# Batch one of a fused attention and mixer kernel: the second pair's q and k turned on TensorE, nine steps masked by VectorE, mixing pair by pair

## The chip, the cores and the metric

The kernel runs on one core of a Trainium2 chip. Its time is the device time of one launch in microseconds, the median over the runs. A profiled execution also has a span, from its first to its last recorded instruction. All times inside an execution are counted from the start of that span.

## What is computed

Block-sparse attention over 4 batches, 8 heads, 768 tokens and a head size of 64, followed by a mixer over the 512 channels. The first half, cut to what matters:

```python
scores = scale * np.matmul(q, k.transpose(0, 1, 3, 2))
# mask: neighbouring blocks of 32 tokens, the first and the last block,
# and three sampled blocks for each block of queries
scores = np.where(mask, scores, -1000000000.0)
attn = exp(scores - max) / sum
x = attn @ v                         # then heads side by side: (4, 768, 512)
```

The second half, with U of 768x32 and V of 32x768, w_ch1 of 512x2048 and w_ch2 of 2048x512:

```python
h = xt @ U @ V                       # xt: x with tokens and channels swapped
u = x + h.transpose(0, 2, 1)
ch = np.maximum(u @ w_ch1, 0.0) @ w_ch2
return u + ch
```

The mask is the same for all batches and heads.

## The kernel before

**Units of work.** Two heads make a pair; there are 4 pairs in a batch (pairs 0 to 3 are batch one, pair 4 begins batch two) and 9 steps in a pair, 144 steps in all, numbered through. A step makes the scores of one 128-key tile against 512 queries for both heads (the first six steps of a pair, two matmuls of 64x512), or of two key tiles against the remaining 256 queries (the last three, four matmuls of 64x256), with keys on the partitions. `score` then lets ScalarE take the exp of the whole 128x1024 PSUM tile into an SBUF tile `e`. `values` multiplies each `e` with v, eight matmuls of 65 columns a step; the 65th column is the sum for the softmax. When half of a pair's queries is complete, `divide` takes the reciprocal on VectorE and writes the normalised half as float32 (`x32`) and float16 (`x16`).

**Two ways to mask.** In a *biased* step two more matmuls (or four, for the 256-wide kind) add -60000 to forbidden scores inside PSUM, from the tiles `bias` and `qhot`. In an unbiased step the exp runs on plain scores, and VectorE afterwards multiplies `e` with a 0/1 `mask` (`apply_masks`), before `values` may read it. `build_bias` makes the bias; `build_allow` and `spread` make the mask in pieces. Before the change steps 2 to 35 are biased; steps 0, 1 and 36 to 143 are masked by VectorE.

**Turning q and k.** q and k come by DMA on SP's queue as float32 (`raw_q`, `raw_k`), are narrowed to float16 (`narrow_part`, `narrow_pair`: tiles `st_q`, `st_k`) and turned so that the head size lies on the partitions (`qT`, `kT`). For pair 0 TensorE turns them (`prepare_part`, `transpose_part`) into PSUM and another engine copies them out; for all later pairs a transposing DMA on SP's queue does it (`transpose_by_dma`, called by `prepare_next` together with the loads of the pair after). SP's queue and POOL's work strictly in order: a transposing DMA that waits for its narrowed source holds up the loads that stand behind it.

**Mixing.** `amix` multiplies `x16` with U, `umix` makes u turned (`uT`, one tile per 128 channels, that is per pair) by adding `x16` turned against the identity and V times the amix result in PSUM, and copies it out. In batches two to four only the last pair is done so; the others add in natural layout (`unat`) and turn by DMA. `channels` then runs the two large layers: `up` (pieces `j`, `part`, `half`; w_ch1 and relu into `tT`) and `down` (w_ch2, added to `x32`, stored).

**Order.** One loop writes down all instructions of all engines, choosing at each turn among the next scores ("qk"), values ("av"), mixing pieces and channel pieces. It keeps a model clock per engine (`clk`; `FIX`, `COL`, `HOP` are its costs in ns) and takes the candidate with the best rank among those that its clock holds to be ready. The clock sets only the order and which engine does a copy (`pick`); on the chip everything waits on semaphores.

**PSUM.** While batch one's attention runs (`ahead[0]` true) PSUM is cut into two score tiles of two banks (`sc`) and four single banks (`one`): accumulators of a pair, transposes, amix and umix. When all of batch one is mixed, `all_to_two` closes these pools and opens one of four two-bank tiles (`two`). So step k's scores wait for the exp of step k-2. The stretch up to this re-cut is called the first stage; it contains the scores and exps of steps 0 to 37.

Batch one is mixed in two groups: pairs 0 to 2 together (one amix of 384 columns and three umix), then pair 3. Pair 3's `divide` is ordered reciprocal, `x16`, `x32` for each half.

## Time and profile before

| | |
|---|---|
| median of three runs | 291.26 us (290.24 to 292.35) |
| the profiled execution | 291.53 us, span 289.70 us |
| TensorE busy, 2791 matmuls | 279.0 us, 96% of the span |
| ScalarE busy | 187.9 us, 65% |
| VectorE busy | 159.8 us, 55% |
| POOL busy | 63.6 us, 22% |
| granted TensorE clock | 1.00 |
| exp of 128x1024 | 106 on `two` (1026 ns mean), 38 on `sc` (1040 ns) |
| mask of 128x1024 on VectorE | 74 and 36 (750 and 752 ns mean) |

How to read it: TensorE's busy share includes the pipelined tails of matmuls, so 96% doesn't say that it never waits inside the first stage. The busy shares are means over stages with different limits; for the first stage the exps of ScalarE and the gaps between them tell more. A line of the timeline gives the start, the length of the merged group, the engine, the source line, what is written from what, how many instructions were merged and, in brackets, how long the engine sat idle before them and what released it. PE is TensorE, ACT ScalarE, DVE VectorE. L413 and L420 are the score and bias matmuls, L428 the exp, L504 the values, L603 and L608 the copies of `uT`, L665 and L694 the channel layers.

### The profile page before, as it was taken

The numbers are of one execution on the slowest core, as the hardware profiler recorded it, in microseconds if no ns is written. First come the engines' busy times: TensorE is split into PE (matmuls) and PEld (weight loads), VectorE is DVE, ScalarE is ACT, GpSimd is POOL, SyncE is SP. The second block draws the span as 40 slices with busy tenths as digits, with TensorE's granted clock in tenths as the row PEclk, the third lists the DMA queues.
The fourth block names the chain that finished last, engine by engine and source line by source line (L and its number), as shares of the span: only waits on it lengthen the run. The fifth ranks groups of instructions, "written<-read, shape, count | busy, mean of one in ns | idle before, by whom it ended". The sixth has DMA issues, their size and how long they took to land.

```text
span 289.7 us, 6483 instructions
## 1 busy us (share of the span) xinstructions
PE 279.0 (96%) x2791; PEld 159.1 (55%) x2791; DVE 159.8 (55%) x262; ACT 187.9 (65%) x217; POOL 63.6 (22%) x81
## 2 busy tenths in 40 slices
PE   7998998999899999999999998999999999999995
PEld 2554654566464655566566455566655455565444
DVE  5562256775957665675687666666755743000112
ACT  4898988796957746877965476859786533664000
POOL 4655644501304043004006503004010100000000
PEclk9999999999999999999999999999999999999999
DMA  7799999999952858361626955712110311000122
GB/s 214 193 203 207 237 230 204 281 201 215 156 164 54 242 126 218 98 196 27 141 80 69 268 143 187 217 48 55 29 29 0 102 72 75 0 2 0 54 86 80
DMA packets 52212, 37.68 MB, mean 130 GB/s; under 512 B 33424, under 2 KB 50624, under 8 KB 52184
## 3 DMA queue, kind: packets, MB, share of 16 engines
q1 hardware_dynamic: 46672, 32.71, 43.5%
q0 software_dynamic: 5152, 4.39, 9.6%
q8 instruction: 22, 0.36, 0.6%
q10 hardware_dynamic: 360, 0.17, 0.2%
q14 instruction: 6, 0.05, 0.1%
HBM read 27.59 MB, written 6.29 MB: 117 GB/s over the span
## 4 chain that ended last, share of the span: by engine, by line
PE 86%; ACT 5%; DMA 5%; DVE 1%; issue 1%; POOL 0%; SPq 0%; ACTq 0%; POOLq 0%
PE two L665 29%; PE two L694 28%; PE two L504 9%; PE two L413 8%; ACT e L428 4%; DMA raw_k<-in_k_dram 3%; PE sc L413 3%; PE one L504 2%; DMA kT<-st_k 2%; PE sc L420 2%; PE two L575 1%; PE two L722 1%; PE two L618 1%; PE two L700 1%; ACT uT L608 1%
## 5 line engine op out<-in xcount | busy, mean ns | idle before, releaser
L428 ACT ACTIVATE e<-two 128x1024 f16<-128x1024 f32 x106 | 100.7, 1026 | 19.4 <-PE two L413 19.3
L665 PE MATMUL two<-uT,w1t 128*128 128x256 f16 (+1 forms) x512 | 88.3, 326 | 0.4 <-ACT uT L608 0.2
L694 PE MATMUL two<-w2t,tT 128*128 128x512 f16 x368 | 86.9, 379 | 0.0
L665 PEld LDWEIGHTS <-w1t 128*128 128x128 f16 x512 | 48.2, 98 | 34.9 <-issue 5.7
L461 DVE TENSOR_TENSOR e<-e,mask 128x1024 f16<-128x1024 f16 x74 | 53.4, 750 | 9.3 <-ACT e L428 9.1
L694 PEld LDWEIGHTS <-tT 128*128 128x128 f16 x368 | 33.1, 98 | 39.1 <-issue 5.9
L504 PEld LDWEIGHTS <-e 128*128 128x128 f16 x1152 | 38.3, 97 | 11.8 <-issue 8.4
L682 ACT ACTIVATE tT<-two 128x1024 f16<-128x1024 f32 x31 | 31.7, 1023 | 16.8 <-PE two L665 16.8
L428 ACT ACTIVATE e<-sc 128x1024 f16<-128x1024 f32 x38 | 36.3, 1040 | 4.6 <-PE sc L420 3.5
L708 DVE TENSOR_TENSOR of<-x,two 128x1024 f32<-128x1024 f32 (+1 forms) x12 | 14.1, 1176 | 42.8 <-PE two L700 42.6
L627 POOL CAST x<-x 128x768 f16<-128x768 f32 x9 | 8.1, 900 | 121.9 <-DVE x L624 121.9
L413 PE MATMUL two<-qT,kT 64*128 64x512 f16 (+1 forms) x284 | 29.9, 324 | 2.5 <-DVE uT L603 1.1
L551 ACT CAST x<-x 128x384 f16<-128x384 f32 x24 | 12.3, 512 | 30.1 <-DVE x L537 30.1
L680 DVE TENSOR_SCALAR tT<-two 128x1024 f16<-128x1024 f32 x17 | 20.8, 1225 | 19.7 <-PE two L665 19.7
L413 PEld LDWEIGHTS <-kT 64*128 64x128 f16 x384 | 17.3, 94 | 24.2 <-issue 15.2
L466 DVE TENSOR_TENSOR e<-e,mask 128x1024 f16<-128x1024 f16 x36 | 26.2, 752 | 3.6 <-ACT e L428 3.5
L504 PE MATMUL two<-v,e 128*128 128x65 f16 x864 | 28.2, 193 | 0.0
L413 PE MATMUL sc<-qT,kT 64*128 64x512 f16 (+1 forms) x100 | 16.0, 331 | 1.7 <-DMA kT<-st_k 1.2
L163 POOL CAST st_q<-raw_q 128x768 f16<-128x768 f32 x15 | 12.7, 844 | 22.0 <-DMA raw_q<-in_q_dram 16.1
L154 POOL CAST v<-raw_v 128x768 f16<-128x768 f32 x16 | 14.9, 932 | 5.2 <-DMA raw_v<-in_v_dram 4.8
L163 POOL CAST st_k<-raw_k 128x768 f16<-128x768 f32 x15 | 13.9, 926 | 7.2 <-DMA raw_k<-in_k_dram 6.8
L420 PE MATMUL sc<-qhot,bias 64*128 64x256 f16 (+1 forms) x92 | 14.4, 320 | 0.0
(75 smaller groups left out, 156.1 us busy)
## 6 DMA issues: line engine op xcount, KB each, us to landing
raw_v<-in_v_dram SPq DMA_DIRECT2D x16, 384.0 KB, 5.9
raw_q<-in_q_dram SPq DMA_DIRECT2D x15, 384.0 KB, 4.2
raw_k<-in_k_dram SPq DMA_DIRECT2D x15, 384.0 KB, 4.5
out_dram<-of SPq DMA_DIRECT2D x11, 512.0 KB, 3.3
w1t<-in_moe_w_ch_dram POOLq DMA_DIRECT2D x4, 512.0 KB, 8.8
w2t<-in_moe_w_ch_dram POOLq DMA_DIRECT2D x4, 512.0 KB, 10.5
raw_q<-in_q_dram SPq DMA_DIRECT2D x1, 256.0 KB, 2.9
raw_k<-in_k_dram SPq DMA_DIRECT2D x1, 256.0 KB, 4.2
```

The costliest lines, as they stand in the source:

```text
L154: nc.gpsimd.tensor_copy(out=vs[n % VB][:, :, :, 0:D], in_=raw["v", n].rearrange("p h (t d) -> p t h d", d=D))
L163: nc.gpsimd.tensor_copy(out=st, in_=raw[name, n].rearrange("p h (t d) -> p t h d", d=D))
L413: nc.tensor.matmul(sc[:, h, at : at + nq], kT[h * D : (h + 1) * D, g * P : (g + 1) * P], qT[h * D : (h + 1) * D, q0 : q0 + nq], start=True ...
L420: nc.tensor.matmul(sc[:, h, at : at + nq], biasf[h * D : (h + 1) * D, g : S : NT], qhot[h * D : (h + 1) * D, q0 : q0 + nq], start=False, s ...
L428: nc.scalar.activation(out=e, in_=sc, func=AF.Exp, scale=0.125)
L461: nc.vector.tensor_mul(out=e, in0=e, in1=m)
L466: nc.vector.tensor_mul(out=ev, in0=ev, in1=m)
L504: nc.tensor.matmul(acc[1][hf][:, t % (NT // 2), h, :], e[:, h, at + t * P - q0 : at + t * P - q0 + P], vt[:, g, h, 0 : D + 1], start=(done ...
L665: nc.tensor.matmul(pt[:, half, at : at + nq], w1t[:, c, (4 * j + i) * P : (4 * j + i + 1) * P], uT[c][:, q0 : q0 + nq], start=(c == 0), st ...
L680: nc.vector.tensor_scalar_max(out=dst, in0=pt, scalar1=0.0)
L682: nc.scalar.activation(out=dst, in_=pt, func=AF.Relu)
L694: nc.tensor.matmul(po[:, i], tT[j // 4][:, j % 4, t * P : (t + 1) * P], w2t[:, j, :], start=(j == 0), stop=False,)
```

## The change

Ten edits, all on batch one's stage but for the last lines of `up`, which concern every batch:

1. Of pair 0's k, columns 2 and 3 are narrowed by VectorE instead of POOL, ahead of `bias`, and copied out of PSUM by VectorE instead of ScalarE.
2. Pair 1's q and k are turned on TensorE at steps 6 and 7; its two transposing DMAs go. `spread` follows at step 7 instead of 3, its second part at step 14 instead of 16.
3. Steps 21 to 23 and 27 to 32 become unbiased and are masked by VectorE.
4. Pair 0's values are taken in the order of steps 2 to 8, 0, 1 (before: 2 to 5, 0, 1, 6 to 8).
5. Each half of a pair is divided when its own matmuls are complete.
6. Pair 3's two `x32` products are put off (`later`) until the last `uT` piece has been copied.
7. Batch one is mixed by single pairs, and `umix` is cut into a piece of 512 and one of 256 columns.
8. The first channel pieces (`j` and `part` 0) multiply channels 0 to 2 for both halves, and channels 3 in the second piece.
9. The planner stops scoring at step 37 until the re-cut, and ranks scores otherwise.
10. Model costs: `FIX` of ScalarE 180 instead of 400 ns, `HOP` by engine.

The diff, cut to its core:

```diff
-    def build_bias():
+    def count_allowed():
...
+    def build_bias():
...
-    FIX = {"ACT": 400, "DVE": 350, "POOL": 250}
+    FIX = {"ACT": 180, "DVE": 350, "POOL": 250}
-    HOP = 150
+    HOP = {"ACT": 350, "DVE": 150, "POOL": 150}
...
     (prepare_next)
-            transpose_by_dma(n + 1)
-            t_qk[n + 1] = t + 9000
+            if n > 0:
+                transpose_by_dma(n + 1)
+                t_qk[n + 1] = t + 9000
...
+    with_bias = {*range(2, 2 * SPP + 3), *range(2 * SPP + NT, 3 * SPP), *range(3 * SPP + NT, SPB)}
...
-        biased = 2 <= si < SPB
+        biased = si in with_bias
...
     (apply_masks)
+            if ahead[0] and masks[0][1] >= SPB:
+                break
...
-    avq = [*range(2, NT), 0, 1, *range(NT, NSTEP)]
+    avq = [*range(2, SPP), 0, 1, *range(SPP, NSTEP)]
...
     (values)
-        before, acc[0] = acc[0], acc[0] + len(sis)
-        if ahead[0] and before < NT <= acc[0]:
-            divide(n, 0, acc[1][0], t)
+        acc[0] += len(sis)
+        for hf in range(2):
+            if acc[2][hf] == each and (ahead[0] or acc[0] == SPP):
+                acc[2][hf] = None
+                divide(n, hf, acc[1][hf], t)
...
     (divide, pair 3)
             t_x[n] = times(x16[:, p, ts])
+            if ahead[0]:
+                later.insert(0, lambda: drop(times(x32[:, ts, c])))
+                return
...
-        def umix(c):
+        def umix(c, q0=0, q1=S):
...
+            if c == NPR - 1 and q1 == S:
+                while later:
+                    later.pop()()
...
+            elif b > 0:
+                pieces.append((ready, lambda c=c: umix(c)))
+            else:
+                pieces.append((ready, lambda c=c: umix(c, 0, QA)))
+                pieces.append((ready, lambda c=c: umix(c, QA, S)))
...
     (up)
+            pieces, need = [half], tm["uT"]
+            cs = range(NC)
+            if j == 0 and part == 0:
+                pieces, cs = range(2), [range(NC - 1), range(NC - 1, NC)][half]
+                need = max(tm[c] for c in cs)
             if part < 2:
-                todo = [(2 * part + half, 0, QA, 0)]
+                todo = [(x, 2 * part + x, 0, QA, 0) for x in pieces]
...
-    narrow_part("k", 2, NT, nc.gpsimd.tensor_copy)
+    narrow_part("k", 4, NT, nc.gpsimd.tensor_copy)
...
+    count_allowed()
+    narrow_part("k", 2, 4, nc.vector.tensor_copy)
     build_bias()
...
-    groups = deque([(0, 0, NPR - 1), (0, NPR - 1, NPR)])
-    groups.extend((b, p, p + 1) for b in range(1, B) for p in range(NPR))
+    groups = deque((b, p, p + 1) for b in range(B) for p in range(NPR))
...
-        if step < NSTEP:
+        if step < (SPB + 2 if ahead[0] else NSTEP):
...
-                hurry = step < SPB and clk["ACT"] < now + 1500
-                rank = 2 if chan else 0.5 if hurry else 2.5 if step < SPB else 4
+                hurry = ahead[0] and clk["ACT"] < now + 1500
+                rank = 2 if chan else 4 if not ahead[0] else 2.5 if not hurry else 0.5 if step < SPB else 0.9
...
-                prepare_part("k", 2, 4, "ACT", 16500.0)
-                prepare_part("k", 4, NT, "DVE", 16500.0)
+                prepare_part("k", 2, 4, "DVE", 15500.0)
+                prepare_part("k", 4, NT, "DVE", 16000.0)
...
+            if step == 6:
+                prepare_part("q", 0, NT, "DVE", 25500.0, 1)
+            if step == 7:
+                t_qk[1] = prepare_part("k", 0, NT, "DVE", 25500.0, 1)
                 spread(0, 2, 0, 4, "DVE")
-            if step == 16:
+            if step == 14:
                 spread(2, NT, 0, 4, "DVE")
```

More of the change, by code (lines that the diff above doesn't have):

```diff
@@ L198 @@
     mask = consts.tile([P, NT, S], FP16)
-    def build_bias():
+    allow = consts.tile([P, NB], FP32)
+    def count_allowed():
         sbf = consts.tile([P, 3], FP32)
         nc.vector.tensor_copy(out=sbf, in_=sbi[:, 0::2])
-        allow = consts.tile([P, NB], FP32)
         for r in range(3):
@@ L299, in new_qkT, with transpose_part @@
         return dst
-    def transpose_part(name, t0, t1, evict):
-        st = staged[name, 0]
+    def transpose_part(name, n, t0, t1, evict):
+        st = staged[name, n]
         if t0 == 0:
-            first[name] = new_qkT(name, 0)
+            first[name] = new_qkT(name, n)
         pt = slot(FP16)[:, 0, 0 : (t1 - t0) * P].rearrange("c (t p) -> c t p", p=P)
@@ L331, in on @@
         clk[eng] = max([clk[eng], *needs]) + FIX[eng] + COL[eng] * cols * rate
-        return clk[eng] + HOP
+        return clk[eng] + HOP[eng]
     def on_pe(cols, kind, *needs):
@@ L377, with prepare_part @@
     sc_free = [0.0, 0.0]
-    def prepare_part(name, t0, t1, eng, need):
+    def prepare_part(name, t0, t1, eng, need, n=0):
         cols = (t1 - t0) * P
         t = on_pe(cols * 1.3, "full", take(), need)
-        transpose_part(name, t0, t1, COPY[eng])
+        transpose_part(name, n, t0, t1, COPY[eng])
         t = on(eng, cols, t, rate=0.55 if eng == "DVE" else 1.0)
@@ L438, in score @@
             masks.append((t, si, e))
-            t_e[si] = max(t, clk["DVE"]) + FIX["DVE"] + COL["DVE"] * 1024 * 0.55 + HOP
+            t_e[si] = max(t, clk["DVE"]) + FIX["DVE"] + COL["DVE"] * 1024 * 0.55 + HOP["DVE"]
         etiles[si] = e
@@ L511, in values @@
         t = on_pe(len(sis) * 8 * AVC, "full", need)
-        before, acc[0] = acc[0], acc[0] + len(sis)
-        if ahead[0] and before < NT <= acc[0]:
-            divide(n, 0, acc[1][0], t)
+        acc[0] += len(sis)
[3 more added lines that the diff above has]
+                divide(n, hf, acc[1][hf], t)
         if acc[0] == SPP:
-            if not ahead[0]:
-                divide(n, 0, acc[1][0], t)
-            divide(n, 1, acc[1][1], t)
             del accs[n]
+    later = []
     def divide(n, hf, acc, t):
@@ L577, in amix @@
                 )
-            tt = on_pe(NT * max(np_ * P, 200), "full", lt["x16"], take())
+            tt = on_pe(NT * max(np_ * P, 140), "full", lt["x16"], take())
             eng = pick(np_ * P, tt)
@@ L582, in amix @@
             give(lt["a16"])
-        def umix(c):
-            uT[c] = utp.tile([P, S], FP16, tag="uT", name="uT")
-            cs = slice(c * P, (c + 1) * P)
-            both, ends = None if ahead[0] else slot(), []
-            for q0, q1 in ((0, QA), (QA, S)):
-                pu = (slot()[:, 0] if ahead[0] else both[:, q0 // QA])[:, 0 : q1 - q0]
-                for t in range(q0 // P, q1 // P):
+        def umix(c, q0=0, q1=S):
+            if q0 == 0:
+                uT[c] = utp.tile([P, S], FP16, tag="uT", name="uT")
+            pu = slot().rearrange("c i q -> c (i q)")
+            for r0, r1 in [(q0, q1)] if ahead[0] else [(0, QA), (QA, S)]:
+                for t in range(r0 // P, r1 // P):
@@ L592, in umix @@
                     nc.tensor.matmul(
                         pu[:, t * P - q0 : (t + 1) * P - q0], x16[:, c, t, :], id16,
-                        start=(t * P == q0), stop=False,
+                        start=(t * P == r0), stop=False,
                     )
+                on_pe((r1 - r0) * 1.1, "full", lt["x16"], take())
                 nc.tensor.matmul(
-                    pu, a16[:, cs], Vt.rearrange("r t p -> r (t p)")[:, q0:q1],
-                    start=False, stop=True,
-                )
@@ L600, in umix @@
-                tt = on_pe((q1 - q0) * 2.15, "full", lt["a16"], take())
-                if ahead[0]:
-                    eng = pick(q1 - q0, tt)
-                    COPY[eng](out=uT[c][:, q0:q1], in_=pu)
-                    ends.append(on(eng, q1 - q0, tt))
-                    give(ends[-1])
-            if not ahead[0]:
-                eng = pick(S, tt)
-                COPY[eng](out=uT[c], in_=both.rearrange("c i q -> c (i q)")[:, 0:S])
-                ends.append(on(eng, S, tt))
-                give(ends[-1])
@@ L611, in umix @@
-            tm["uT"] = max(tm.get("uT", 0.0), *ends)
+                    pu[:, r0 - q0 : r1 - q0], a16[:, c * P : (c + 1) * P],
+                    Vt.rearrange("r t p -> r (t p)")[:, r0:r1], start=False, stop=True,
+                )
+                tt = on_pe(r1 - r0, "full", lt["a16"])
+            eng = pick(q1 - q0, tt)
+            COPY[eng](out=uT[c][:, q0:q1], in_=pu[:, 0 : q1 - q0])
+            end = on(eng, q1 - q0, tt)
+            give(end)
+            tm[c] = max(tm.get(c, 0.0), end)
@@ L613, in unat @@
+            tm["uT"] = max(tm.get("uT", 0.0), end)
+            if c == NPR - 1 and q1 == S:
+                while later:
+                    later.pop()()
         def unat(c):
@@ L633, in unat @@
             )
-            tm["uT"] = max(tm.get("uT", 0.0), tt + 10500)
+            tm[c] = tt + 10500
+            tm["uT"] = max(tm.get("uT", 0.0), tm[c])
         pieces = [(lambda: max(take(), lt["x16"]), amix)]
-        pieces += [
-            (lambda: max(take(), lt["a16"]),
-             lambda c=c: unat(c) if natural(b, c) else umix(c))
-            for c in range(p0, p1)
-        ]
+        for c in range(p0, p1):
+            ready = lambda: max(take(), lt["a16"])
+            if natural(b, c):
+                pieces.append((ready, lambda c=c: unat(c)))
+            elif b > 0:
[3 more added lines that the diff above has]
+                pieces.append((ready, lambda c=c: umix(c, QA, S)))
         return pieces, (b, uT, x32, a16, tm)
@@ L658, in up @@
             pt = hold["up"]
+            pieces, need = [half], tm["uT"]
[3 more added lines that the diff above has]
+                need = max(tm[c] for c in cs)
             if part < 2:
-                todo = [(2 * part + half, 0, QA, 0)]
+                todo = [(x, 2 * part + x, 0, QA, 0) for x in pieces]
             else:
-                todo = [(2 * half + i, QA, QB, i * QB) for i in range(2)]
-            for i, q0, nq, at in todo:
-                for c in range(NC):
+                todo = [(half, 2 * half + i, QA, QB, i * QB) for i in range(2)]
+            for x, i, q0, nq, at in todo:
+                for c in cs:
                     nc.tensor.matmul(
-                        pt[:, half, at : at + nq],
+                        pt[:, x, at : at + nq],
                         w1t[:, c, (4 * j + i) * P : (4 * j + i + 1) * P], uT[c][:, q0 : q0 + nq],
@@ L669, in up @@
                     )
-            tt = on_pe(NC * 512, "full", tm["uT"], hold["at"])
+            tt = on_pe(len(todo) // (1 + (part == 2)) * len(cs) * 512, "full", need, hold["at"])
             if half == 0:
@@ L740, in channels @@
         pieces = [
-            ((lambda: max(tm["uT"], take())) if half == 0 else free,
+            ((lambda: max(*(tm[c] for c in range(NC - 1)), take())) if j == part == half == 0
+             else (lambda: max(tm["uT"], take())) if half == 0 else free,
              lambda j=j, part=part, half=half: up(j, part, half), half == 0)
@@ L811 @@
         now = clk["PE"]
-        if chan or not mixes or clk["DVE"] <= now:
+        if chan or ahead[0] or not mixes or clk["DVE"] <= now:
             apply_masks(now + 300)
         cands = []
-        if step < NSTEP:
+        if step < (SPB + 2 if ahead[0] else NSTEP):
             n = step // SPP
@@ L818 @@
                 free = sc_free[0] if ahead[0] else take()
-                size = 3 if chan else 1
+                size = 1 if not chan else 3
                 if chan:
                     free = max(take(i + 1) - 512 * i for i in range(size + chan[0][2]))
-                hurry = step < SPB and clk["ACT"] < now + 1500
-                rank = 2 if chan else 0.5 if hurry else 2.5 if step < SPB else 4
+                hurry = ahead[0] and clk["ACT"] < now + 1500
+                rank = 2 if chan else 4 if not ahead[0] else 2.5 if not hurry else 0.5 if step < SPB else 0.9
                 if rank == 4:
```

## Prediction

> **What bounds the kernel now.** I read the page first, then busy time by stretch, then the chain of work that ended last, then the timelines of ScalarE and TensorE, then TensorE's waits. The chain, from 12 us on (start, length, what):

> ```profile
> 12.79 6.36 DMA raw_k<-in_k_dram
> ...
> 20.31 4.37 DMA kT<-st_k
> 24.68 0.04 issue
> 24.73 0.39 PE sc L413 x2
> 25.11 0.22 PE sc L420 x2
> 25.33 0.35 PE one L504 x8
> ...
> 47.51 0.61 DVE uT L603
> 48.12 0.04 issue
> 48.16 0.82 PE two L413 x6
> ```

> The first stage (batch one's attention) ends when the first matmul on the re-cut PSUM starts, at 48.16. It contains a wait for the k of pair 2 (load, narrowing, transposing DMA). In the stage ScalarE runs one exp of 128x1024 per step:

> ```profile
> 8.94 1.02 ACT L428 ACTIVATE e<-sc 128x1024 f16<-128x1024 f32 x1 [0.73 <-PE sc L420]
> 10.18 14.19 ACT L428 ACTIVATE e<-sc 128x1024 f16<-128x1024 f32 x15 [0.21 <-PE sc L420]
> 25.43 10.19 ACT L428 ACTIVATE e<-sc 128x1024 f16<-128x1024 f32 x11 [1.07 <-PE sc L420]
> 35.82 1.94 ACT L428 ACTIVATE e<-sc 128x1024 f16<-128x1024 f32 x2 [0.20 <-PE sc L420]
> 38.35 2.15 ACT L428 ACTIVATE e<-sc 128x1024 f16<-128x1024 f32 x2 [0.59 <-PE sc L420]
> ...
> 45.16 1.02 ACT L428 ACTIVATE e<-sc 128x1024 f16<-128x1024 f32 x1 [0.36 <-PE sc L413]
> ```

> Back to back an exp takes 14.19/15 = 0.946 or 10.19/11 = 0.926; I use 0.935. A biased step costs TensorE 0.32 + 0.22 (scores, bias) + 0.35 (eight value matmuls), 0.89 to 0.92, so the two engines are nearly equal and anything added to TensorE opens a gap on ScalarE: so from 35.8 on, where mixing begins. After 48.16 TensorE is the bound; these are all its waits to the end (engine, line waited for, us, times, longest):

> ```profile
> PE two L413 <- DVE uT L603: 1.1, 1, 1.1
> PE two L413 <- ACT e L428: 1.1, 3, 0.5
> PE two L592 <- ACT e L428: 0.5, 1, 0.5
> PE two L665 <- ACT uT L608: 0.2, 1, 0.2
> PE two L413 <- ACT tT L682: 0.2, 1, 0.2
> ```

> So what the change is worth is how far 48.16 moves, plus at most the 2.0 us of the other waits.

> **The change, part by part.** I walked the new order of instructions step by step (steps count from 0; step 3's exp stood at 10.18, step 36's at 45.16). Durations from the chain of before: biased score 0.54 (512 wide) or 0.57 (two 256 halves), unbiased 0.32, eight values 0.35, sixteen 0.59, an umix of 512 columns 0.33 + 0.22, of 256 0.11 + 0.11, six 128-wide amix matmuls 0.34 from start to start (100.17 to 100.51).

> *Start.* k's columns 2 and 3 are narrowed by VectorE (a 256-column copy took 0.29 there) and 4, 5 by POOL (256 columns 0.40, where 512 took 1.02), and both PSUM copies go to VectorE, so none waits for ScalarE's first two exps, which end at 7.95. Before, the copy there ended at 8.22 and step 2's scores began at 8.27. Now VectorE finishes the bias at about 6.9 (0.29 later), the first k copy at 7.5, the scores 0.61 later, the exp at 8.2: 0.74 earlier. Step 3's exp comes to 9.45, 0.73 earlier. Bounds: 0 (the part of raw_k, which landed at about 6.05, comes late) and 0.8.

> *Second pair on TensorE.* Two times six transposes replace two transposing DMAs. The trace has no six in a row; two take 0.12 in the chain, four 0.44 as records. I take 0.06 each, 0.34 per six; bounds 0.34 and 0.66 (0.11 each). Their sources were ready at 9.5 and 10.5, they are wanted at 11.4 and 12.7. [...] The two copies out of PSUM (768 columns; 512 took 0.42) I take at 0.6 on VectorE. In step 7 TensorE does values 0.35 + transposes 0.34 + scores 0.56 = 1.25 against 0.935: ScalarE idles 0.31.

> On SP's queue the loads of pair 2 stood behind the two transposing DMAs and were issued at 12.22 to 13.3. Now they wait only for raw's buffers (6.9 to 8.4). With the same 6.4 us to landing raw_k is there at 14, narrowed at 15, turned by 20; step 18 wants it at 24. The 1.07 us gap goes. Pair 3 follows the same way (turned by 30, wanted at 32.6). On POOL its narrowing now stands behind the x16 copy of pair 1's first half; that is inside the 30.

> *Masks.* Steps 21 to 23 and 27 to 32 lose their two bias matmuls, 9 x 0.22 = 2.0 us of TensorE, and cost VectorE 9 x 0.68 = 6.1 us. VectorE was busy 3.53 and 2.66 us of the ten in 20 to 30 and 30 to 40, and in the walk each mask ends before its values come up. But the masks of steps 0 and 1 now stand behind the second pair's copies: first fill of the mask 2.32 us from 13.75, masks done at 16.7 and 17.35. The values that need the first come up at 16.3, and step 11's scores are queued behind them: 0.22 of gap. Without VectorE's idle time each late mask would delay scores by its 0.68.

> *Mixing pair by pair.* One 384-wide amix (1.08) and three umix stood at 36.6 to 44.4. Now three 128-wide amix (3 x 0.44 with the change of tile shape) and the umix pieces lie among steps 15 to 34, in the room that the unbiased steps leave (0.32 + 0.35 = 0.67 against 0.935). In the walk ScalarE idles 0.6 in steps 13 to 20, 0.2 at step 24, 0.2 at step 34.

> Sum: step 36's exp at 9.45 + 33 x 0.935 + 0.31 + 0.22 + 0.6 + 0.2 + 0.2 = 41.9 (to 0.05), against 45.16.

> *Hand-over.* It grows from 3.0 to 4.35 us. The last values end at 42.6, division 0.7, second half of amix 43.65. The a16 copy on ScalarE queues behind step 37's exp (to 43.9) and takes 0.27, umix 0.25, uT's copies 0.6. VectorE copies uT's second piece until 45.15 and then does both x32 products (0.56 + 0.50), now put last. The first channel matmul is to overlap the wait for the last uT, but its PSUM tile is the first of the re-cut pool, and in the compiled order it waits for the uT copy and for the second x32 product. So at this place the change doesn't do what it says; the matmul starts at 46.25. All values, scores and umix due by then are the same as at 48.16 before: gain 1.9.

> *Later batches.* The planner's new constants are no instructions; the order they leave is the same but for small swaps, with 31 relus on ScalarE and 17 on VectorE as before. The first pieces take channels 0 to 2 of both halves first. In batch four that covers the 0.24 that TensorE idles for uT at 244.79 (six matmuls of 0.22 against three). The rest I leave at 0, bounds -0.6 and +0.8 (one more or fewer of the waits shown).

> Total 1.9 + 0.24 = 2.15: span 289.70 to 287.55. The profiled execution took 291.53, 1.83 more than its span, hence 289.4. The median of the runs is 291.26, 0.27 below it, so I predict 289.1. With upper prices instead (0.66 for six transposes, 0.50 for an amix and 0.70 for sixteen values, as their records have them) step 36's exp comes to 42.9, the channel matmul to 47.3, the sum to 1.1.

> **Rivals.** (A) ScalarE paces the whole stage, gapless: 33 x 0.935 from 9.45 gives 40.3, 1.6 us earlier again, 287.5. For it: 15 and 11 exps without a gap. Against: a biased step leaves TensorE only 0.02 to 0.05 of room. (B) Upper prices, 291.26 - 1.1 = 290.2. For it: the gaps of 0.59, 0.42 and 0.36 as soon as mixing was on TensorE. Against: the nine lightened steps. (C) Slower: batch two's first k is late. Its narrowing on POOL stands behind the x16 copy of pair 2's first half, itself behind the masks of steps 21 to 23, so it ends at about 36.1 (35.4 before), while step 36's scores move up from 44.7 to 41.2. All transposed tiles of k, time to landing:

> ```profile
> DMA to landing us min/median/max: 2.8/2.9/8.9
> ```

> This one landed in 4.1 before, which leaves 1.0 us. At 8.6 (the q tile issued at 43.09 took 8.3) it is at 44.7, 3.5 late, and everything behind step 36's scores with it: 289.1 + 3.5 = 292.6. Slower than before from a landing of 7.3 us on. For it: DMA shares of 1.07 to 1.26 between 32 and 44. Against: two transposing DMAs fewer and earlier loads. (D) The transposes don't pipeline: 12 x 0.28 (record of a pair) = 3.4 instead of 0.7, 291.8. [...]

> **How the numbers follow.** Forecast 0.43, own range 287.8 to 290.2 (1.1 less gain or 1.3 more, from the bounds of start, transposes and later waits, not all at once); A 0.15; B 0.22; C 0.12; D 0.03; something unnamed 0.05. The range 286.9 to 292.6 takes in A and C and leaves out some 0.15. About what a measurement of this kernel can tell is 1%, 2.9 us: below 288.35 lie A and 0.4 of the forecast, 0.33; above 294.2 only C's far end and the unnamed, 0.09; between, 0.58.

> **What would show it.** Right: step 3's exp near 9.5; no DMA of kT in the chain before 36 us; step 36's exp at 41.5 to 42.9; first matmul after the re-cut at 46 to 47.3, released by VectorE's x product; no wait for uT in batch four. Wrong: ScalarE gaps of over 0.5 in steps 9 to 33, a wait for kT at step 36 (C), or waits after the hand-over above 2.6 us in sum, which would mean that the planner's new constants moved more than I saw.

## The result, and the profile after

The changed kernel takes 295.08 us in the median (293.51 to 296.19), the kernel before beside it 291.53 us: a ratio of 1.0121, with 95% certainty between 1.0082 and 1.0160. It is slower by 3.5 us, where 289.1 was forecast. (Here and below a median is over all executions of a run; a ratio leaves out the few executions that took over 1.5% longer than the fastest of their kernel.) The profiled execution took 296.19 us, with a span of 294.2 us.

In the changed kernel L311 is the transposes on TensorE and L314 their copies out of PSUM, L243 the fill of the mask, L471 the product with the mask, L420 and L427 scores and bias, L435 the exp, L514 the values, L548 the products with the reciprocal (`x`), L689 the first channel layer; L163 and L154 are POOL's narrowing. POOL is GpSimd. In the experiments the same lines stand a few lines higher or lower.

The chain of work that ended last, of the changed kernel (start, length, what):

```profile
13.65 0.56 DVE kT L314
14.21 4.08 DVE mask L243 x6
...
18.39 0.70 DVE e L471
...
40.12 5.87 DMA kT<-st_k
...
50.17 0.94 DVE x L548 x2
...
51.25 2.72 PE two L689 x6
```

The DMA that brings the k of pair 2 is gone from it, as forecast. In its place stands VectorE's first fill of the mask, 4.08 us long where 2.32 was taken. The first stage ends at 51.25 instead of 48.16 (46.25 forecast), and the six channel matmuls there take 2.72 us. ScalarE's timeline of the changed kernel:

```profile
10.00 4.00 ACT L435 ACTIVATE e<-sc 128x1024 f16<-128x1024 f32 x4 [0.21 <-PE sc L427]
14.20 3.77 ACT L435 ACTIVATE e<-sc 128x1024 f16<-128x1024 f32 x4 [0.20 <-PE sc L427]
20.14 1.02 ACT L435 ACTIVATE e<-sc 128x1024 f16<-128x1024 f32 x1 [2.16 <-PE sc L427]
21.40 1.02 ACT L435 ACTIVATE e<-sc 128x1024 f16<-128x1024 f32 x1 [0.24 <-PE sc L427]
23.37 19.55 ACT L435 ACTIVATE e<-sc 128x1024 f16<-128x1024 f32 x20 [0.94 <-PE sc L427]
...
46.53 1.02 ACT L435 ACTIVATE e<-sc 128x1024 f16<-128x1024 f32 x1 [0.35 <-PE sc L420]
```

The forecast gave a late mask 0.22 us. It cost 2.16 + 0.24 + 0.94 us between 18 and 23.4. After that twenty exps follow in one group, that is with no idle time above 0.15 us between them (19.55 / 20 = 0.978 us each; the forecast had 0.935 each and 0.8 us of gaps on this stretch, 19.5 in all): the middle of the stage takes the time that was forecast. TensorE's waits from 12 us to the end, in the changed kernel (engine, line waited for, us, times, longest):

```profile
PE one L514 <- DVE e L471: 2.3, 2, 2.0
PE two L689 <- DVE x L548: 1.5, 1, 1.5
...
PE sc L420 <- DMA kT<-st_k: 0.7, 1, 0.7
```

Two large waits, then, and a small one for the k of pair 4. Each of the two large ones is followed by a stretch at half clock (granted clock 0.50). Busy time by stretch, of the changed kernel (length; busy us and instructions of PE, PEld, DVE, ACT, POOL; granted clock; DMA share; GB/s):

```profile
17.05:20.47 3.42, 1.43 (x26) 0.83 (x24) 2.58 (x5) 1.26 (x3) 0.96 (x1) 1.00 0.76 162
20.47:23.88 3.41, 3.41 (x34) 1.61 (x34) 3.19 (x10) 2.22 (x3) 1.07 (x2) 0.50 0.77 270
...
47.77:51.19 3.42, 1.49 (x16) 0.85 (x14) 2.00 (x5) 1.76 (x3) 0.78 (x1) 1.00 1.13 297
51.19:54.60 3.41, 3.35 (x10) 1.02 (x12) 1.19 (x2) 0.00 (x0) 1.82 (x4) 0.50 0.56 122
```

In two stretches of 3.41 us the granted clock is 0.50, and in the 3.41 us ahead of each TensorE was busy for only 1.43 and 1.49 us. The six executions order themselves by this: 293.51 us at a mean clock of 0.999, 294.52 to 295.33 at 0.992 to 0.994, and 295.85 and 296.19 at 0.987. (One stretch of 3.41 us at 0.50 takes 0.006 off the mean of 290 us.) In the kernel before, 13 executions at 0.992 to 0.994 have a median of 292.93 and 63 at 0.997 or more one of 291.55. An estimate from these two differences, 2.5 us for two stretches and 1.4 for one: one such stretch costs some 1.3 to 1.4 us.

### The profile page after: what moved, and what is told of

Same layout as the page of the kernel before. It is cut to its first block, busy times and chain, and to the rows that moved or that the text cites. A ratio compares the mean times of both kernels' runs of the same rounds, so it can differ in the third digit from the quotient of the medians.

```text
span 294.2 us, 6509 instructions
## 1 busy us (share of the span) xinstructions
PE 281.7 (96%) x2797; PEld 160.2 (54%) x2797; DVE 168.1 (57%) x276; ACT 188.1 (64%) x215; POOL 65.0 (22%) x83
## 4 chain that ended last, share of the span: by engine, by line
PE 87%; ACT 4%; DVE 3%; POOL 2%; DMA 2%; issue 1%; ACTq 0%; POOLq 0%; DVEq 0%
PE two L689 29%; PE two L718 27%; PE two L514 9%; PE two L420 8%; ACT e L435 3%; PE sc L420 2%; PE one L514 2%; DMA kT<-st_k 2%; PE one L264 2%; DVE mask L243 1%; PE two L589 1%; PE sc L427 1%; PE two L746 1%; PE two L631 1%; POOL mask L243 1%
## 5 line engine op out<-in xcount | busy, mean ns | idle before, releaser
L435 ACT ACTIVATE e<-two 128x1024 f16<-128x1024 f32 x106 | 100.7, 1026 | 24.4 <-PE two L420 24.2
L689 PE MATMUL two<-uT,w1t 128*128 128x256 f16 (+1 forms) x512 | 90.3, 329 | 2.0 <-DVE x L548 1.5
L689 PEld LDWEIGHTS <-w1t 128*128 128x128 f16 x512 | 48.3, 98 | 37.2 <-issue 9.4
L471 DVE TENSOR_TENSOR e<-e,mask 128x1024 f16<-128x1024 f16 x83 | 60.8, 759 | 9.4 <-ACT e L435 9.2
L514 PEld LDWEIGHTS <-e 128*128 128x128 f16 x1152 | 38.5, 98 | 12.6 <-issue 6.2
L435 ACT ACTIVATE e<-sc 128x1024 f16<-128x1024 f32 x38 | 36.8, 1029 | 6.6 <-PE sc L427 4.3
L706 ACT ACTIVATE tT<-two 128x1024 f16<-128x1024 f32 x31 | 31.7, 1022 | 13.7 <-PE two L689 13.3
L732 DVE TENSOR_TENSOR of<-x,two 128x1024 f32<-128x1024 f32 (+1 forms) x12 | 14.1, 1175 | 41.9 <-PE two L724 41.8
L420 PE MATMUL two<-qT,kT 64*128 64x512 f16 (+1 forms) x284 | 30.1, 327 | 1.3 <-ACT e L435 1.1
L420 PEld LDWEIGHTS <-kT 64*128 64x128 f16 x384 | 17.4, 94 | 24.8 <-issue 17.7
L514 PE MATMUL two<-v,e 128*128 128x65 f16 x864 | 28.2, 193 | 0.0
L476 DVE TENSOR_TENSOR e<-e,mask 128x1024 f16<-128x1024 f16 x36 | 25.6, 736 | 4.2 <-ACT e L435 4.1
L163 POOL CAST st_q<-raw_q 128x768 f16<-128x768 f32 x15 | 12.5, 836 | 30.4 <-issue 16.6
L420 PE MATMUL sc<-qT,kT 64*128 64x512 f16 (+1 forms) x100 | 16.8, 349 | 1.4 <-DMA kT<-st_k 0.7
L514 PE MATMUL one<-v,e 128*128 128x65 f16 x288 | 13.9, 198 | 2.3 <-DVE e L471 2.3
L163 POOL CAST st_k<-raw_k 128x768 f16<-128x768 f32 x15 | 14.7, 980 | 4.7 <-DMA raw_k<-in_k_dram 4.7
L154 POOL CAST v<-raw_v 128x768 f16<-128x768 f32 x16 | 14.7, 919 | 3.4 <-DMA raw_v<-in_v_dram 3.3
```

Source lines behind the costliest of these rows:

```text
L154: nc.gpsimd.tensor_copy(out=vs[n % VB][:, :, :, 0:D], in_=raw["v", n].rearrange("p h (t d) -> p t h d", d=D))
L163: nc.gpsimd.tensor_copy(out=st, in_=raw[name, n].rearrange("p h (t d) -> p t h d", d=D))
L420: nc.tensor.matmul(sc[:, h, at : at + nq], kT[h * D : (h + 1) * D, g * P : (g + 1) * P], qT[h * D : (h + 1) * D, q0 : q0 + nq], start=True ...
L435: nc.scalar.activation(out=e, in_=sc, func=AF.Exp, scale=0.125)
L471: nc.vector.tensor_mul(out=e, in0=e, in1=m)
L476: nc.vector.tensor_mul(out=ev, in0=ev, in1=m)
```

## The experiments

Why did the fill take so long? In the kernel before it began at 9.72 us, beside two of POOL's casts with a pause of 0.17 us between them. VectorE's and POOL's timelines of the kernel before:

```profile
9.70 0.83 POOL L163 CAST st_k<-raw_k 128x768 f16<-128x768 f32 x1 [0.24 <-DMA raw_k<-in_k_dram]
9.72 2.32 DVE L240 COPY mask<-allow_k 128x192 f16<-128x192 f16 x6
10.70 0.93 POOL L154 CAST v<-raw_v 128x768 f16<-128x768 f32 x1 [0.17 <-DMA raw_v<-in_v_dram]
```

Now it begins at 14.13, beside POOL's narrowing of pair 2, which the earlier loads brought there, and the copy of `Vt` right behind it. POOL's timeline, and the fill copies from the view of the tile `mask` (durations in ns, least/median/longest), of the changed kernel:

```profile
14.28 0.96 POOL L163 CAST st_q<-raw_q 128x768 f16<-128x768 f32 x1
15.20 0.84 POOL L163 CAST st_k<-raw_k 128x768 f16<-128x768 f32 x1
15.99 0.87 POOL L154 CAST v<-raw_v 128x768 f16<-128x768 f32 x1
16.81 1.20 POOL L294 COPY Vt<-Vn 128x768 f16<-128x768 f16 x1
```

```profile
L243 DVE COPY mask<-allow_k x12: 234/333/2079, 14.1 to 23.4; 128x160 f16<-128x160 f16 x4, 128x320 f16<-128x320 f16 x4, 128x192 f16<-128x192 f16 x2, 128x384 f16<-128x384 f16 x2
```

One copy took 2.08 us, the shortest 0.23. The long one lies from 16.10 to 18.18 and ends just behind POOL's copy of `Vt` (18.01). My theory has two causes: (1) VectorE's copies take longer beside POOL's casts and copies, so the masks are late; (2) the two x32 products put off behind the last `uT` copy hold the re-cut PSUM, and TensorE idles long enough for the clock to drop. Rivals: the late mask comes from the fill's new place alone; the late hand-over comes from pair 4's k (rival C).

**POOL stands still during the fill.** It reads one column of the filled mask before it narrows pair 2 (in `prepare_next`):

```diff
+            if n == 1:
+                nc.gpsimd.tensor_copy(out=hold_pool, in_=mask[:, 1, QA - 1 : QA])
             narrow_pair(n + 1)
```

> The changed kernel, but POOL reads one element of the first mask fill (a one-column copy) before it narrows pair 2, so that it stands still while VectorE fills the mask. Theory 1 (POOL's narrowing, which the earlier loads moved under the fill, stretches VectorE's six copies from 2.3 to 4.1 us; the wait for the masks of steps 0 and 1 then idles TensorE for 2.0 us and its clock is halved for 3.5 us): the fill takes 1.5 to 2.3 us, TensorE waits at most 0.7 us, the clock stays at 1.00 in 20 to 24 us, and the time falls by 2 to 3 us. Rival (the fill is slow where it stands, or stands too late, whatever POOL does): the fill stays near 4 us, the time within 0.7 us of the changed kernel.

Measured: 292.04 us, ratio to before 0.9996 (0.9968 to 1.0024), 3.0 us below the changed kernel. VectorE's and ScalarE's timelines:

```profile
13.65 1.03 DVE L244 COPY mask<-allow_k 128x192 f16<-128x192 f16 x6
```

```profile
13.72 25.25 ACT L438 ACTIVATE e<-sc 128x1024 f16<-128x1024 f32 x26 [0.20 <-PE sc L430]
```

At the same place and in the same order the six copies take 1.03 us, and 26 exps follow in one group. So it is POOL's work beside the fill, not the fill's place alone. The hand-over is as in the changed kernel (1.54 us idle, then half clock).

**The fill at its old place**, step 3, ahead of pair 1's copies:

```diff
             if step == 3:
...
+                spread(0, 2, 0, 4, "DVE")
             if step == 7:
-                spread(0, 2, 0, 4, "DVE")
```

> The changed kernel with the first mask fill back at step 3 on VectorE's queue, ahead of the copies of the second pair's q and k. If its place behind those copies is what makes the masks late: masks of steps 0 and 1 done at about 14, no wait of TensorE for them, clock at 1.00, time lower by 2 to 3 us. Rival: the q and k copies now come late (the fill takes up to 3.5 us beside POOL's narrowing of pair 1), step 9's scores wait for kT, and less than half of that is gained.

Measured: 292.78 us, ratio 1.0015 (0.9979 to 1.0051). The fill takes 2.33 us from 9.81, pair 1's copies come just in time (0.2 us of wait), 26 exps are in one group. A second way to the same end: the wait goes when the masks are early, however that is brought about.

**The x32 products ahead of the uT copies** (in `amix`):

```diff
             give(lt["a16"])
+            while later:
+                later.pop()()
```

> The changed kernel, but pair 3's two x32 products stand on VectorE's queue ahead of the copy of the last uT piece, in the time in which VectorE waits for umix. Theory 2 (put last, they alone stretch TensorE's wait at the hand-over to 1.5 us, and the half clock that follows costs another 1.5 us): the first channel matmul comes 1.0 us sooner, TensorE idles about 0.6 us, its clock stays at 1.00, the first six channel matmuls take 1.3 instead of 2.7 us; time lower by 2 to 2.5 us. Rival (the wait is for the uT copy, the products hide behind it): under 0.5 us.

Measured: 292.47 us, ratio 1.0018 (0.9983 to 1.0052), 2.6 us below the changed kernel. TensorE's timeline:

```profile
50.74 0.82 PE L420 MATMUL two<-qT,kT 64*128 64x512 f16 x6 [0.52 <-DVE uT L619]
```

TensorE now waits 0.52 us, for `uT`, and runs on at full clock (1.00); the early mask wait is there as in the changed kernel (2.1 us in sum). (The order has shifted too: score matmuls now stand first on the re-cut PSUM, where the channel matmuls did.)

**TensorE kept busy at the hand-over**, with nothing earlier:

```diff
+                spin = two_banks("sc")
+                for _ in range(7):
+                    nc.tensor.matmul(spin[:, 0, :], warm[:, 0:P], warm[:, 0:512], start=True, stop=True)
                 all_to_two()
```

> The changed kernel with seven matmuls of 128x512 on zeros (0.22 us each) between the last umix and the re-cut, on a score tile that is free; their results are read by nobody. Theory 2: the first channel matmul still starts near 51.2 us, but its clock stays at 1.00 and the first six take 1.3 instead of 2.7 us; time lower by 1.5 to 2 us. Rival (the slow matmuls come from something else than the idle time, such as the weights arriving): the six still take 2.7 us and the time stays.

Measured: 293.20 us, ratio 1.0052 (1.0018 to 1.0086). TensorE's timeline:

```profile
50.04 1.46 PE L689 MATMUL two<-uT,w1t 128*128 128x512 f16 x6
```

The six matmuls that took 2.72 us take 1.46. In this profile the early wait (2.5 us in sum) was followed by no drop of the clock either (1.00 throughout); the last section has the busy times.

**Both busy fillers.** The same seven, and six matmuls that add zeros ahead of the values of step 0:

```diff
+        if sis[0] == 0:
+            for _ in range(6):
+                nc.tensor.matmul(rest[0], warm[:, 0:P], warm[:, 0:390], start=False, stop=False)
```

> The changed kernel with TensorE kept busy at both idle places: six matmuls of 390 columns with zeros (nothing is added to the accumulators) ahead of the values of step 0, where it waits for the mask, and the seven dummy matmuls of e3_spin_at_handover. Nothing that is waited for comes earlier, so this takes the clock's part of the loss away and leaves the waits. If each stretch at half clock costs 1.2 us by itself: no stretch at half clock before 290 us in the profile, the mask wait ends as late as before (1 us of ScalarE idle near 19 to 20 us), and 292.5 to 293.5 us, about 2 us below the changed kernel. Rival (the half clock only fills time in which TensorE would wait anyway): 294.5 to 295.2 us.

Measured: 293.67 us, ratio 1.0067 (1.0031 to 1.0104), the mean clock of the profiled execution 1.0, ScalarE's gap still 1.75 us. That is 1.4 us below the changed kernel, and about what the changed kernel's own execution at 0.999 took (293.51). But the run has four executions, its interval overlaps that of the changed kernel, and it is no faster than the filler at the hand-over alone (293.20). So that some 1.4 us of what was lost is the clock, and the rest the waits themselves, is an estimate and not shown.

**Both cures together** (POOL held, x32 early):

> The changed kernel with the two edits together: POOL stands still while VectorE fills the mask for the first time, and the two x32 products of pair 3 are ordered ahead of the copies of uT. Theory (two separate causes, contention at the fill and the idle TensorE at the hand-over): the savings add up, 3.0 + 2.6 us off 295.1, that is 289 to 289.5 us; fill of six copies 1.0 us, ScalarE without a gap from 13.7 to 39 us, idle time of TensorE at the hand-over below 0.6 us, and no stretch with a granted clock below 0.9. Rival (one and the same loss, seen at two places: what one edit saves is waited for at the other place): 291.5 to 292.5 us, no better than either alone.

Measured: 289.74 us (289.06 to 290.46), ratio 0.9934 (0.9912 to 0.9957). The savings nearly add up: 3.0 and 2.6 alone, 5.3 together. The 26 exps from 13.68 on are in one group. TensorE's timeline:

```profile
46.33 0.82 PE L423 MATMUL two<-qT,kT 64*128 64x512 f16 x6 [0.52 <-DVE uT L622]
```

The stage ends at 46.33, where the prediction had 46.25; that the two meet is partly luck, as the next section shows. This version is faster than both kernels, by 0.7% of the one before.

**The first x16 of pairs 1 and 2 on VectorE**, so that POOL narrows the k of pair 4 sooner (both cures kept, as in the next two):

```diff
             eng = pick(nt * P, t, engines=("POOL", "DVE" if n < NPR else "ACT"))
+            if n in (1, 2) and hf == 0:
+                eng = "DVE"
```

> As e5_both, and the x16 copies of the first halves of pairs 1 and 2 are made by VectorE instead of POOL, so that POOL narrows the k of pairs 3 and 4 earlier. Rival C of the prediction (pair 4's k late because its narrowing stands behind x16 on POOL): transposing DMA of pair 4's k issued 1 to 2 us earlier, the wait for kT ahead of step 36 (0.4 to 1.2 us in the earlier runs) gone, time 0.4 to 1 us below e5_both. If the wait is set by the DMA's own length and by the loads beside it: issue earlier, landing not earlier, same time as e5_both within 0.3 us.

A miss: 291.17 us at full clock and 295.67 to 297.51 in three more executions, with mean clocks of 0.982 to 0.993; too uneven for a ratio. VectorE's timeline and TensorE's waits, in an execution of 296.64 us:

```profile
31.49 2.75 DVE L474 TENSOR_TENSOR e<-e,mask 128x1024 f16<-128x1024 f16 x1
```

```profile
PE sc L423 <- DMA kT<-st_k: 3.2, 1, 3.2
PE one L517 <- DVE e L474: 2.0, 1, 2.0
```

POOL had its three casts for pair 4 in a row now, from 31.32 to 33.68, and the mask product that began in them (0.67 us in the version with both cures) ended at 34.24: cause (1) at a second place. And the transposing DMA of pair 4's k, issued 2.1 us earlier (34.00 instead of 36.15), took 13.0 us to land instead of 5.9. Issued earlier, it came in later. More landings of this DMA, issue to landing: 36.40 in 4.1 (before), 40.12 in 5.9 (after), 36.15 in 5.9 (both cures). What sets its length is open; the loads of pair 5 and of w_ch1 that are on their way with it are the suspects, and they were not moved alone.

**All of steps 2 to 35 biased** again:

```diff
-    with_bias = {*range(2, 2 * SPP + 3), *range(2 * SPP + NT, 3 * SPP), *range(3 * SPP + NT, SPB)}
+    with_bias = {*range(2, SPB)}
```

> As e5_both, but steps 21 to 23 and 27 to 32 are biased on TensorE again, as before the change (nine masks fewer on VectorE, 18 or more bias matmuls back on TensorE). The prediction's term: 9 x 0.22 = 2.0 us of TensorE that is needed for mixing; then step 36's exp comes 1 to 2 us later than in e5_both, and the time is 1 to 2 us longer. Rival (ScalarE sets the pace at 0.98 us an exp and TensorE has the room anyway): gaps between the exps below 0.5 us in sum, same time as e5_both within 0.4 us.

Measured: 289.57 us, ratio 0.9925 (0.9897 to 0.9954). In the time of the kernel the nine steps masked by VectorE are worth nothing that shows. In the profiles they are worth something at first: from step 7's exp to step 33's it is 26.54 us here (25 exps in 25.25 us from 13.99) and 25.44 with both cures. But there TensorE then waits 0.8 us for the k of pair 4, which here is in time, and of the 1.1 us 0.4 are left at the first matmul on the re-cut PSUM. What the nine steps would bring with an earlier k of pair 4, no run shows.

**Mixing in the old two groups:**

```diff
-    groups = deque((b, p, p + 1) for b in range(B) for p in range(NPR))
+    groups = deque([(0, 0, NPR - 1), (0, NPR - 1, NPR)])
+    groups.extend((b, p, p + 1) for b in range(1, B) for p in range(NPR))
```

> As e5_both, but batch one is mixed in two groups as before the change: pairs 0 to 2 together, then pair 3 (umix still in pieces of 512 and 256 columns). If mixing pair by pair is what lets the mixing hide among steps 15 to 34: gaps of ScalarE from 36 us on as before (0.2 to 0.6 us each, 1 to 2 us in sum), and 1 to 2 us longer than e5_both. If TensorE has the room there in any case: same as e5_both within 0.4 us. It could also be shorter by 0.2 to 0.4 us, since one amix of 384 columns has fewer instructions than three of 128.

Measured: 291.27 us, ratio 0.9964 (0.9932 to 0.9995), against 0.9934 with single pairs. The intervals overlap; four executions at full clock took 290.11 to 290.77, so mixing by single pairs brings 0.5 us (from these four) to 1.5 (from the median), and the profile shows a wait of 1.7 us for pair 4's k. Not settled beyond that.

**Pair 1 turned by DMA again**, all biased, x32 early, the fill at step 3, POOL not held:

```diff
-            if n > 0:
-                transpose_by_dma(n + 1)
-                t_qk[n + 1] = t + 9000
+            transpose_by_dma(n + 1)
+            t_qk[n + 1] = t + 9000
...
-            if step == 6:
-                prepare_part("q", 0, NT, "DVE", 25500.0, 1)
-            if step == 7:
-                t_qk[1] = prepare_part("k", 0, NT, "DVE", 25500.0, 1)
```

> As e7_all_biased (all of steps 2 to 35 biased, x32 ahead of the uT copies), but pair 1's q and k are again turned by the two transposing DMAs and the mask is first filled at step 3, as before the change; POOL is not held. What stays of the change is the mixing by single pairs, the order of values and divisions, and the hand-over. If turning pair 1 on TensorE is what takes the 1.07 us wait for the k of pair 2 away, as the prediction has it: that wait is back near 24 us, ScalarE sits idle 0.5 to 1.1 us there, and the time is 0.6 to 1.1 us above e7_all_biased, about 290.4. Rival (the twelve transposes and two copies cost about what they save): no wait over 0.3 us for kT at 24 us, or an earlier step 36, and 289.3 to 289.8 us.

Measured: 293.42 us, ratio 1.0056 (1.0032 to 1.0079): 3.9 us above the version with all steps biased, far more than the 0.6 to 1.1 expected. The wait for pair 2's k is not what returned. TensorE's waits:

```profile
PE one L588 <- POOL x L564: 1.9, 2, 1.7
PE sc L419 <- DMA kT<-st_k: 1.4, 1, 1.4
```

The second is for the k of pair 1 itself: its transposing DMA is issued at 11.68, and step 9's scores wait for it until 16.17. (In the kernel before, where it was issued at 10.89 and step 3's exp stood 0.6 us later, nothing waited for it.) Counted from step 3's exp, step 9's comes 1.2 us later than with all steps biased.

The first comes from POOL. The loads of pair 2 are issued at 13.02 to 14.12 again, behind the two transposing DMAs. POOL narrows pair 2 at 18.09 and pair 3 at 28.39 (24.20 with both cures), and the x16 copies that mixing by single pairs wants stand behind that in POOL's queue; one holds `amix` up for 1.7 us, and a stretch at half clock follows (32.56 to 35.97). By step 25's exp 4.4 us are lost. So turning pair 1 on TensorE pays by some 1.2 us through its own k and by some 3 through what it frees on SP's queue and POOL; here mixing by single pairs needs it.

Edits 1, 4, 5, 8, 9 and 10 were not taken back one by one; what each is worth is open.

## Why the prediction was wrong, point by point

- *Masks*: this is the first step that failed. "First fill of the mask 2.32 us from 13.75" took the duration from a place where two of POOL's casts lay beside it, with a pause of 0.17 us between them; at its new place the fill lay beside three casts of pair 2 and the copy of `Vt` in a row, without a pause. The casts came there by the earlier loads, which the prediction itself had worked out ("raw_k is there at 14, narrowed at 15"). Measured 4.16 us. The masks were done at 19.1 instead of 16.7, and the gap of 0.22 became 3.3 with the slow clock behind it. Freed of POOL the fill takes 1.03. Whether VectorE stands still beside POOL or only runs slower was not shown; the copy of 2.08 us and, with x16 on VectorE, the product of 2.75 us each lay beside more than one of POOL's instructions.
- *Hand-over*: the second step that failed. The releaser was named rightly (the second x32 product) and so was the growth: 4.72 us from step 36's exp instead of 4.35. But its 1.54 us of idle TensorE were priced as time alone; the clock dropped, and the matmuls behind took 1.26 us more (2.72 against 1.46). Putting x32 ahead makes the hand-over 3.71 us (42.62 to 46.33).
- *Clock*: no term of the sum lets it drop. The profiled execution before stood at 1.00, and I took that for a property of the kernel.
- *Start*: from step 0's exp to step 3's it is 3.56 us instead of 4.17, a gain of 0.61 for 0.73. Step 0's exp itself came 0.43 later, at 6.44, within what the profiled executions of all these kernels differ by (5.64 to 6.73).
- *Transposes*: six took 0.33 to 0.35 us and the copies out 0.56, as forecast; rival D is out. Pair 2's k came in time, also as forecast. What turning pair 1 on TensorE is worth was set too low, as the last experiment shows.
- *The 9 x 0.22 us* of the unbiased steps, forecast as room for mixing: 1.1 us by step 33 in the profiles, but nothing that shows in the time.
- *Rival C*: it was there, small. Pair 4's k landed in 5.87 us and TensorE waited 0.68; the chain runs through it, but it is not what made the kernel slower. With both cures it is the largest wait left in the stage (0.8 us).
- *Later batches*: from the first matmul on `two` to the end 241.5 us before, 241.4 with the filler at the hand-over, 241.0 with x32 early; 0.24 was forecast.

With the two failed steps cured the kernel takes 289.74 us, 5.3 below the changed kernel and 0.6 from the forecast. This nearness is partly luck. The cured kernel isn't the one that was forecast: the forecast counted 4.35 us of hand-over with the x32 products last, and with them ahead it takes 3.71. Step 36's exp, in turn, stands at 42.62 instead of 41.9, and the two offset each other. So of the 6.0 us by which the forecast was wrong about 4.7 (5.3 less that 0.64) are put down to the two steps. The profile of the changed kernel agrees: 3.1 us more than forecast at the masks (3.34 less 0.22), 0.4 at the hand-over and 1.3 of slow matmuls behind it. The rest is open.

## What to carry to other kernels

When an edit brings work on one engine forward, look what it now lies beside on the engines that were seen to hold it up: a duration read beside two of POOL's casts (2.32 us) didn't hold beside four of its instructions in a row (4.16). Price an idle TensorE twice, once for the wait and once for the clock that may drop behind it (1.54 and 1.26 us at the hand-over here), and judge that from several executions, since one and the same kernel, the one before, had a mean clock of 0.992 to 0.994 in 13 executions and of 0.997 or more in 63. And an edit's worth can lie in the queue that it frees and not in the wait that it was aimed at.

## What the runs showed of the hardware

```profile
45.28:48.69 3.41, 1.99 (x20) 0.95 (x18) 3.22 (x5) 2.38 (x5) 1.17 (x2) 1.00 1.20 224
```

That kernel, too, has executions with one stretch at half clock, as the 13 at a mean clock of 0.992 to 0.994 show, and the 2.5 us of wait in the run with the filler at the hand-over was followed by no half clock: the grid cut it in two (2.01 and 2.61 us busy). Once, in the run with x16 on VectorE, the half clock lasted two intervals (48.49 to 55.31 us).

A VectorE copy of 128x192 took 2.08 us beside POOL's cast and copy, where the six copies of that fill take 0.24 to 0.31 each while POOL is held, and a mask product of 0.67 took 2.75 beside three casts. It goes both ways: with POOL held during the fill, two of its casts lie beside mask products and take 1.29 and 1.28 us instead of 0.83. And a transposing DMA that was issued 2.1 us earlier landed 4.9 us later (47.03 instead of 42.09).
